# Early query sums for tiles 0 and 1, second-norm statistics by bn_stats, and new instruction orders in an attention-and-GLU block

## The chip, the cores and the metric

The kernel runs on one core of one Trainium2 chip. Its time is the device time of one execution in microseconds; the time before is 205.43 us, the median of 3 runs (205.39 to 205.56). The engines are PE (TensorE, with its weight loads shown as PEld), DVE (VectorE), ACT (ScalarE), POOL (GpSimd) and SP (SyncE, which only issues DMAs here). Each has its own queue of instructions and takes them in order. An instruction that waits for another engine holds up all that is queued behind it on its own.

## The reference

One transformer block on x of 2048 rows by 448 columns, bf16. First comes linear attention with 16 heads of 28 columns, and then a gated layer of width 1792:

```python
qkv = layernorm(x) @ wqkv
pq, pk = einsum(q, w_phi), einsum(k, w_phi)          # per head, 28 by 28
phi_q = concat([softmax(pq), softmax(-pq)])          # phi_k likewise
kv, z = einsum(phi_k, v), sum over rows of phi_k
o  = (phi_q @ kv) / (phi_q . z + 1e-6)
h  = x + o @ wo
g, u = layernorm(h) @ w_gate, layernorm(h) @ w_up
out = h + (sigmoid(g) * u) @ w_down
```

## The kernel before

The 2048 rows lie as 16 tiles of 128 rows. Every piece of work is an "op" with a name, an engine, and the keys of what it reads and writes (`Graph.op`). The engines' orders are written out by hand in the table ORDER, one list of op names for each engine. `emit` walks these lists, and puts a semaphore wait wherever an op needs what another engine, a DMA, or a nearby op of its own engine writes. So the rows of an engine's timeline stand in the order of its list, and each can be named from it; the names below are those of the list, with the tile number at the end (`ek4` is tile 4).

The head (to about 47 us) works as follows. A tile of x comes in (`x`), bn_stats and bn_aggr give its mean and variance (`bst`, `agg`), POOL makes the reciprocal root (`ve1`, `pow1`, with `nm1` and `nb1`), and `xn` writes the normed tile. `xn` may stand on ACT, DVE or POOL. A transpose follows (`xT`), for tiles 0 to 3 on PE with an evacuation `xTe`, for the others by a DMA that SP issues. There are three buffers for the normed tile, so `xn` of tile t waits for the transpose of tile t-3. PE multiplies by the folded key weights and by the value weights: `pva`, `pvb` for one tile from tile 4 on (`ppa` to `vvb` for tiles 0 to 3), into PSUM banks t%2 and 2+t%2. The a part and the b part use opposite halves of the array. ACT takes the exponentials of the key projection with both signs (`ek`, two instructions), ACT or DVE copies the values (`v1`), DVE sums the exponentials by head (`ss`, a tensor_reduce) and inverts the sums (`rs`). `phi` is the product of exponentials and inverse sums, a tensor_tensor on POOL or DVE, into three buffers. PE adds phi transposed times values into banks 6 and 7 (`kva`, `kvb`). `kvz` A to D masks that result into SBUF; `kvzones` writes a column of ones of each head beforehand, from `mask2`, whose two columns are the parity of the partition. `w2m1` and `w2e1` fold the query weights, which need the four transposed loads `ld_q`. `pqa`, `pqb` project the queries of four tiles at once, in two halves, and `eq` takes their exponentials with both signs in two instructions.

The tail of the attention, per tile: `num` (16 small matmuls of eq with kvz, into two banks) gives numerators, denominators and, by the ones column, the sums of the query exponentials. On DVE, `rsm` inverts the negative-sign sum, `qq` is the ratio of sums, `b` scales, `c` adds, `rden` inverts the denominator, and `o` (DVE or POOL) divides. Then `oT` transposes, `woa` and `wob` project with wo for two tiles, `h` adds x. For tiles 0 and 1 x is added on PE, by an identity matmul, and `h` is an ACT copy that accumulates the row sum. `sq` (ACT) accumulates the squares, `nm`, `ve`, `pow2` make mean and reciprocal root, `hn` norms, `hT` transposes (on PE for tiles 0 and 1). From there on PE works on `ga`, `gb` (gate and up, first for tiles 0 and 1), `d..` (down), with the attention of the later tiles between.

The places that the text speaks of: the list ORDER; `kvzones`, `xnorm`, `ekv` (`ek`, `ss`, `rs`, `phi`), `pq` (the function `eqf` with both exps), `kvmask`, `num`, `resid`, `wout`, and PROGRAM, which sets the order in which the ops of the tail are recorded.

## Time and profile before

| what | us |
|---|---|
| median of 3 runs | 205.43 |
| the profiled execution | 205.5 |
| its span, first to last instruction | 203.7 |
| PE busy | 197.6 (97%) |
| DVE busy | 135.9 (67%) |
| ACT busy | 96.5 (47%) |
| POOL busy | 56.8 (28%) |
| granted TensorE clock | 1.00 |

The shares are means over stages that differ. By windows of 4 us, DVE is busy 4.00 us in each window from 20 to 40, POOL 2.38 to 4.00 and ACT 3.43 to 4.00, and PE 3.31 to 4.00. From 96 us on PE is busy 4.00 us in nearly each window, DVE 0 to 3.9, POOL mostly 0. A row of the timeline shows the start in us, the duration in us, the engine, the line of the kernel, the operation, what it writes and reads with shapes, the number of instructions merged in it, and in square brackets the idle time before it with what ended that. A busy PE is not PE at its peak: matmuls overlap, and two that use opposite halves of the array run side by side (a pair of 448 columns starts every 0.19 us, though each shows 0.35).

### The profile page before, as it was taken

Reading aid. Unit: us, or ns where it says so; the run is one execution under the profiler, and the core shown is the slowest. Engines: PE = TensorE matmul, PEld = TensorE weight load, DVE = VectorE, ACT = ScalarE, POOL = GpSimd, SP = SyncE. Lnnn points to the kernel's source line nnn. Section 1 sums busy time; section 2 is a strip of 40 time slices with the busy share of each in tenths; the row PEclk is TensorE's granted clock in tenths of the full one; section 3 lists DMA queues with packets and bytes.
Section 4 is the critical chain, followed back from the end, with each engine's and each line's share of the span. In section 5 each row is a group of like instructions: output and inputs, shape, how many; then the busy total and the mean of one; then the engine's idle time right before and its main releaser. Section 6 shows DMA issues by size and latency. Waiting matters only on the chain.

```text
span 203.7 us, 5832 instructions
## 1 busy us (share of the span) xinstructions
PE 197.6 (97%) x2476; PEld 109.8 (54%) x2476; DVE 135.9 (67%) x329; ACT 96.5 (47%) x194; POOL 56.8 (28%) x98
## 2 busy tenths in 40 slices
...
GB/s 151 318 140 122 55 80 55 245 309 345 196 52 55 65 89 28 55 81 0 3 0 80 122 29 26 3 74 24 58 40 56 3 0 3 0 0 138 0 0 90
DMA packets 32866, 16.25 MB, mean 80 GB/s; under 512 B 25096, under 2 KB 31944, under 8 KB 32840
## 3 DMA queue, kind: packets, MB, share of 16 engines
...
q8 instruction: 19, 0.31, 0.7%
...
q14 instruction: 7, 0.06, 0.1%
...
## 4 chain that ended last, share of the span: by engine, by line
PE 78%; DVE 9%; POOL 4%; DMA 3%; ACT 2%; issue 1%; SPq 1%; POOLq 0%
PE psum L298 73%; PE psum L875 5%; DMA x_sb<-in_A_x_dram 3%; DVE c_sb L746 1%; DVE b_sb L743 1%; POOL rst L516 1%; DVE st L503 1%; DVE xn_pad L532 1%; DVE ss L634 1%; POOL phi L644 1%; DVE rsm L740 1%; ACT xn_pad L529 1%; SPq L397 1%; DVE o_pad L752 1%; ACT v L489 0%
## 5 line engine op out<-in xcount | busy, mean ns | idle before, releaser
L298 PE MATMUL psum<-xnT,wg_sb 64*128 64x512 bf16 (+1 forms) x490 | 93.3, 333 | 0.4 <-DVE rsm L740 0.3
L298 PE MATMUL psum<-xnT,wu_sb 64*128 64x512 bf16 (+1 forms) x490 | 93.2, 333 | 0.0
L847 ACT ACTIVATE sg_sb<-psum 128x512 bf16<-128x512 f32 (+1 forms) x70 | 35.0, 511 | 91.2 <-PE psum L298 90.7
L848 DVE SCALAR_TENSOR_TENSOR hhT<-sg_sb,psum 128x512 bf16<-128x512 bf16 (+1 forms) x70 | 38.9, 576 | 53.9 <-ACT sg_sb L847 53.2
L298 PEld LDWEIGHTS psum<-xnT,wg_sb 64*128 64x128 bf16 x490 | 44.4, 94 | 23.8 <-DVE hhT L848 4.7
L298 PEld LDWEIGHTS psum<-xnT,wu_sb 64*128 64x128 bf16 x490 | 44.4, 94 | 13.4
L298 PE MATMUL psum<-wd_sb,hhT 64*128 64x448 bf16 x336 | 36.8, 349 | 0.0
L298 PEld LDWEIGHTS psum<-wd_sb,hhT 64*128 64x128 bf16 x336 | 17.2, 94 | 15.0 <-DVE x_sb L774 0.6
L644 POOL TENSOR_TENSOR phi<-hhT,rs 128x896 bf16<-128x896 bf16 x14 | 23.3, 1688 | 2.4 <-DVE rs L640 1.9
L298 PE MATMUL psum<-Wk,xnT 64*128 64x448 bf16 x112 | 22.5, 350 | 0.5 <-ACT Wk L489 0.2
L298 PE MATMUL psum<-wv_sb,xnT 64*128 64x448 bf16 x112 | 22.5, 351 | 0.1
L782 POOL TENSOR_SCALAR ve<-ssq 128x1 f32<-128x1 f32 x14 | 3.0, 212 | 65.2 <-ACT junk L779 65.0
L634 DVE TENSOR_REDUCE ss<-hhT 128x32 f32<-128x896 bf16 x16 | 16.9, 1059 | 0.1
L298 PE MATMUL psum<-xnT,Wq 64*120 64x512 bf16 x112 | 14.7, 384 | 0.1
L298 PE MATMUL psum<-wo_o,oT 64*128 64x448 bf16 x56 | 13.2, 349 | 0.0
L298 PE MATMUL psum<-wo_e,oT 64*128 64x448 bf16 x56 | 13.1, 349 | 0.0
L875 PE MATMUL psum<-wd_sb,hhT 128*128 128x448 bf16 (+2 forms) x70 | 11.2, 316 | 0.0
L882 DVE SCALAR_TENSOR_TENSOR x_sb<-psum,x_sb 128x448 bf16<-128x448 f32 (+2 forms) x17 | 9.4, 592 | 2.2 <-PE psum L875 1.6
L779 ACT ACTIVATE junk<-x_sb,sum 128x448 bf16<-128x448 bf16 x16 | 10.5, 658 | 0.0
L503 DVE BATCH_NORM_STATS2 st<-x_sb 128x6 f32<-128x448 bf16 x16 | 9.4, 607 | 1.7 <-DMA x_sb<-in_A_x_dram 1.6
L298 PEld LDWEIGHTS psum<-Wk,xnT 64*128 64x128 bf16 x112 | 7.6, 94 | 5.4 <-PE psum L298 0.5
L746 DVE TENSOR_TENSOR c_sb<-b_sb,psum 128x464 bf16<-128x464 bf16 x16 | 10.1, 633 | 0.4
...
## 6 DMA issues: line engine op xcount, KB each, us to landing
...
```

What stands on the lines that cost most here:

```text
L298: p = e.matmul(o, lhsT=w, rhs=r, start=st, stop=sp, tile_position=(row, 0))
L397: return op(eng, name, lambda e: e.dma_start(dst, src), r=r, w=w, dma="in" if eng == "sp" else "ain", nring=48 if eng == "sp" else 8, kb=kb)
L503: op("dve", "bst%d" % t, lambda e: e.bn_stats(st1[:, t, :], x_sb[:, t, :]), r=[("x", t)], w=[("st1", t)])
L634: op("dve", "ss%d" % t, lambda e: e.tensor_reduce(ss[:, s, :].rearrange("p (b h) -> p b h", h=2), eks.rearrange("p b (d h) -> p b h d", h= ...
L644: return e.tensor_tensor(phi[:, sp, :, :, :].rearrange("p b a n -> p (b a) n")[:, :, 0:56].rearrange("p b (d h) -> p b d h", h=2), eks.rea ...
L746: op("dve", "c%d" % t, lambda e: e.tensor_tensor(h3(c_sb), h3(b_sb), OPv[:, :, :, 0:EV], ALU.add), r=K("b") + BB, w=K("c"))
L779: op("act", "sq%d" % t, lambda e: e.activation(junk[:, t % 2, :], h_sb[:, t, :], ACT.Square, bias=sum2[:, t:t + 1], scale=-float(D), accum ...
L782: op(("pool", "dve"), "ve%d" % t, lambda e: e.tensor_scalar(ve2[:, t:t + 1], ssq2[:, t:t + 1], 1.0 / D ** 3, EPS, op0=ALU.mult, op1=ALU.ad ...
L847: op("act", "sig" + nm, lambda e: e.activation(sg_sb[:, k, 0:N], bk(bg)[:, 0:N], ACT.Tanh, scale=0.5), r=[B(bg)], w=[("sg", k)])
L848: op("dve", "hh" + nm, lambda e: e.scalar_tensor_tensor(out=hhT[(t0 // 4) % NHH][:, ff, ns], in0=sg_sb[:, k, 0:N], scalar=1.0, in1=bk(bu)[ ...
L875: p = e.matmul(bk(b)[:, lo:hi], lhsT=hb[:, ff, TS(t)], rhs=wd_sb[:, ff, lo:hi], start=ff == 0, stop=ff == FT - 1)
L882: op("dve", "fin%d%s" % (t, nm), lambda e: e.scalar_tensor_tensor(out=h_sb[:, t, lo:hi], in0=bk(b)[:, lo:hi], scalar=0.5, in1=h_sb[:, t, l ...
```

## The change

Four edits, and orders that go with them.

- A new op `qs`: 32 matmuls of `eq` for tiles 0 and 1 with the new two-column tile `par` (mask2 in bf16) give the sums of the query exponentials of both tiles without kvz, in banks 2 and 3. One `rsm0` and one `qq0` then serve both tiles; `rsm1` and `qq1` go. `num` makes them itself from tile 2 on.
- For tiles 0 and 1, `h` is a plain copy on ACT; bn_stats (`bs2`) reads the PSUM bank on DVE before it, bn_aggr (`ag2`) gives mean and variance, `ve` adds epsilon on POOL, and `hn` subtracts the mean on DVE. `sq` and `nm` of these tiles go.
- `eq` is two ops (p and m) in place of one with two instructions.
- The memsets `epsl0`, `epsr0`, `v1ones` stand earlier on POOL.
- In the lists: `xn8` goes from DVE to POOL, `xn10` from DVE to ACT, `xn14` from ACT to POOL, `xn15` from ACT to DVE (`xn9` stays on DVE), `kvzones` from DVE to ACT. `phi8`, `phi12` and `phi14` go from POOL to DVE, `phi10` from DVE to POOL. The `v1` copies are shared out anew. `o2` goes from DVE to POOL, `o6`, `o7` from POOL to DVE. Weight loads move ahead of and between the transposes on SP. PE's order differs from `ppa0` to `dn0_11`.

The lists, up to where the first gate matmuls stand, and the head of the code:

```diff
     "sp": (
-        "x1 x0 ld_k0 x2 ld_k2 x4 x6 ld_v0 x10 ld_v2 x8 ld_q2 ld_q1 ld_q0 x12 ld_q3 xT4 xT5 x14 xT6 xT7 xT8 xT9 "
-        "xT10 xT11 xT12 xT13 xT14 xT15 ld_wg0 ld_wu1 ld_wu3 ld_wd1 ld_wg1 ld_woe0 ld_wu0 ld_woe1 ld_woo0 ld_woo1 "
...
+        "x1 x0 ld_k0 x2 ld_k2 x4 x6 ld_v0 x10 ld_v2 x8 ld_woe1 ld_wu0 ld_q2 ld_q1 ld_q0 ld_wg1 x12 ld_woo1 ld_q3 "
+        "xT4 xT5 x14 xT6 ld_wd2 xT7 xT8 ld_wd5 ld_wg2 xT9 xT10 ld_wd4 ld_wd0 xT11 ld_wd3 xT12 xT13 xT14 xT15 "
+        "ld_woo0 ld_wg3 ld_wg0 ld_woe0 ld_wu3 oT2 ld_wu2 ld_wu1 ld_wd6 oT3 ld_wd1 oT4 oT5 oT6 oT7 hT2 hT3 oT8 oT9 "
...
     "act": (
-        "wphi3 wphi2 wphi1 wphi0 wTe0 wTe1 xT1e xT0e wTe2 w2e0_0 w2e0_1 w2e0_2 w2e0_3 xn3 xn4 ek0 ek1 xn5 v1_0 "
-        "v1_1 xn6 ek2 v1_2 v1_3 ek3 w2e1_1 ek4 v1_4 ek5 v1_5 w2e1_0 v1_6 ek6 xn11 ek7 v1_7 xn12 ek8 xn13 ek9 "
-        "w2e1_3 w2e1_2 ek10 xn14 ek11 xn15 v1_11 ek12 eq0_0 ek13 ek14 ek15 v1_14 eq0_1 kvzB eq1_0 eq1_1 eq2_0 oT0e "
-        "eq2_1 h1 h0 sq1 sq0 eq3_0 eq3_1 sig0_1 sig0_0 sig0_3 sig0_2 sig0_5 sig0_4 sq2 sig0_7 sig0_6 sq3 sig0_9 "
...
+        "wphi3 wphi2 wphi1 wphi0 wTe0 wTe1 xT1e xT0e wTe2 w2e0_0 w2e0_1 w2e0_2 w2e0_3 xn3 par xn4 ek0 ek1 xn5 v1_0 "
+        "xn6 ek2 ek3 v1_2 w2e1_0 v1_3 w2e1_1 ek4 v1_4 w2e1_2 ek5 xn10 ek6 v1_6 xn11 ek7 w2e1_3 ek8 v1_8 xn12 ek9 "
+        "xn13 ek10 v1_10 ek11 v1_11 ek12 kvzones eq0_0p ek13 eq0_0m ek14 ek15 v1_15 v1_14 eq0_1p eq0_1m eq1_0p "
+        "kvzB eq1_0m eq1_1p eq1_1m eq2_0m oT1e eq2_0p eq2_1p eq2_1m h1 h0 eq3_0m eq3_0p eq3_1p eq3_1m sig0_1 "
...
     "pe": (
...
-        "ppa0 warm9 ppb0 vva0 xT3 xT2 vvb0 ppa2 ppb2 vva2 vvb2 w2m1_1 w2m1_0 seed kva0 pva4 kvb0 pvb4 pva5 kva1 "
-        "pvb5 kvb1 pva6 kva2 pvb6 pva7 w2m1_2 w2m1_3 pvb7 pva8 kvb2 kva3 pvb8 kvb3 pva9 kva4 pvb9 kvb4 pva10 kva5 "
-        "pvb10 pva11 kvb5 kva6 pvb11 pqa0_0 pva12 kvb6 kva7 pvb12 kvb7 pqb0_0 kva8 pva13 kvb8 kva9 pvb13 kvb9 "
-        "kva10 pva14 pvb14 kvb10 pva15 kva11 pvb15 pqa0_1 kvb11 kva12 pqb0_1 pqa1_0 kvb12 kva13 kvb13 kva14 kvb14 "
-        "kva15 kvb15 pqb1_0 pqa1_1 num0 num1 pqb1_1 pqa2_0 num2 pqb2_0 pqa2_1 oT0 oT1 pqb2_1 num3 woa0 wob0 num4 "
-        "pqa3_0 pqb3_0 num5 pqa3_1 pqb3_1 hT1 hT0 num6 ga0_1 ga0_0 gb0_1 gb0_0 num7 woa2 ga0_3 ga0_2 gb0_3 gb0_2 "
...
+        "ppa0 warm9 xT3 ppb0 xT2 vva0 vvb0 ppa2 ppb2 vva2 seed vvb2 w2m1_1 w2m1_0 kva0 pva4 kvb0 pvb4 pva5 w2m1_2 "
+        "pvb5 kva1 pva6 kvb1 kva2 pvb6 pva7 kvb2 pvb7 kva3 pva8 w2m1_3 pvb8 pva9 kvb3 kva4 pvb9 kvb4 pva10 pqa0_0 "
+        "pvb10 kva5 pva11 kvb5 kva6 pvb11 pva12 kvb6 kva7 pvb12 kvb7 kva8 pqb0_0 pva13 kvb8 kva9 pvb13 pva14 kvb9 "
+        "kva10 pvb14 pva15 kvb10 kva11 pvb15 pqa0_1 kvb11 kva12 pqb0_1 kvb12 kva13 pqa1_0 kvb13 kva14 pqb1_0 kvb14 "
+        "kva15 kvb15 qs pqa1_1 num0 pqb1_1 num1 pqa2_0 num2 pqb2_0 pqa2_1 oT0 oT1 pqb2_1 num3 woa0 wob0 num4 "
+        "pqa3_0 pqb3_0 pqa3_1 num5 hT1 pqb3_1 hT0 num6 ga0_1 ga0_0 gb0_1 gb0_0 woa2 num7 ga0_3 ga0_2 gb0_3 gb0_2 "
...
     "dve": (
...
-        "bst10 agg11 bst9 bst7 agg6 agg7 agg9 bst8 agg8 agg10 mask2 xT3e xT2e ss0 nm1_8 nm1_6 rs0 ss1 bst13 rs1 "
-        "bst12 ss2 bst14 rs2 agg14 xn8 ss3 agg13 agg12 rs3 xn9 bst15 ss4 agg15 xn10 ve1_12 ss5 rs4 ss6 rs5 ss7 rs6 "
-        "v1_8 ss8 v1_9 rs7 ss9 rs8 v1_10 ss10 rs9 rs10 kvzones ss11 v1_12 rs11 phi10 ss12 v1_13 rs12 ss13 rs13 "
-        "ss14 rs14 v1_15 ss15 rs15 phi15 kvzC kvzD kvzA rsm0 qq0 rsm1 b0 qq1 c0 b1 rden0 c1 rsm2 rden1 qq2 o1 b2 "
-        "c2 oT1e rden2 rsm3 qq3 b3 c3 o2 rden3 rsm4 qq4 b4 c4 ve1 rsm5 qq5 ve0 hn1 rden4 b5 c5 hT1e hT0e rsm6 qq6 "
...
+        "bst11 agg11 agg10 agg7 mask2 bst8 bst6 bst9 agg6 agg8 agg9 ve1_6 xT2e ve1_8 xT3e ss0 v1_1 rs0 ss1 bst13 "
+        "rs1 ss2 bst12 agg13 ss3 agg12 rs2 bst15 bst14 rs3 agg15 agg14 v1_5 xn9 nm1_12 ss4 ss5 rs4 v1_7 ss6 rs5 "
+        "ss7 rs6 ss8 v1_9 rs7 ss9 rs8 rs9 ss10 xn15 phi8 ss11 rs10 v1_12 rs11 ss12 v1_13 rs12 ss13 phi12 rs13 ss14 "
+        "rs14 ss15 phi14 rs15 phi15 kvzA kvzC kvzD rsm0 qq0 b0 c0 b1 rden0 c1 rsm2 rden1 qq2 o1 b2 c2 oT0e rden2 "
+        "rsm3 qq3 b3 c3 rden3 bs2_1 rsm4 ag2_1 qq4 bs2_0 b4 ag2_0 c4 hn1 rden4 rsm5 qq5 hT1e b5 hn0 c5 hT0e rden5 "
...
     "pool": (
-        "neghalf ident0 ident phipad wqpad nm1_1 pow1_1 ve1_0 pow1_0 nm1_2 ve1_2 ve1_3 pow1_3 nm1_3 pow1_2 nb1_3 "
-        "ve1_4 nm1_4 pow1_4 nb1_4 nb1_2 xn2 opad0 ve1_6 pow1_6 ve1_8 v1ones epsl0 epsr0 pow1_8 nb1_6 phi0 nb1_8 "
-        "xn7 phi1 phi2 phi3 nm1_12 pow1_12 nb1_12 phi4 phi5 phi6 phi7 phi8 phi9 phi11 phi12 phi13 phi14 o0 nm1 o3 "
...
+        "neghalf ident0 ident phipad wqpad epsl0 epsr0 nm1_1 pow1_1 ve1_0 pow1_0 nm1_2 ve1_2 ve1_3 pow1_3 v1ones "
+        "nm1_3 pow1_2 nb1_3 ve1_4 nm1_4 pow1_4 nb1_4 nb1_2 opad0 xn2 pow1_6 nm1_6 nb1_6 nm1_8 pow1_8 nb1_8 phi0 "
+        "xn7 xn8 phi1 phi2 ve1_12 phi3 pow1_12 phi4 nb1_12 phi5 phi6 xn14 phi7 phi9 phi10 phi11 phi13 o0 o2 ve1 o3 "
+        "pow2_1 ve0 pow2_0 o4 o5 nm2 nm3 pow2_2 hn2 pow2_3 hn3 o9 pow2_4 ve7 ve5 pow2_7 pow2_5 nm5 ve6 pow2_6 ve8 "
...
-    "pq:0,0,4 pq:0,1,4 kvz pq:1,0,0 pq:1,1,4 pq:2,0,0 num:0 num:1,1,2 ot:0 ot:1 wo:0 pq:2,1,4 pq:3,0,0 num:2 "
+    "pq:0,0,4 pq:0,1,4 qs:2 kvz pq:1,0,0 pq:1,1,4 pq:2,0,0 num:0 num:1,1,2 ot:0 ot:1 wo:0 pq:2,1,4 pq:3,0,0 num:2 "
...
+        par = sb("par", [P, 2])
+        st2 = sb("st2", [P, 2, 6], f32)
+        mv2 = sb("mv2", [P, 2, 2], f32)
...
+        op(("dve", "act"), "par", (lambda e: e.tensor_copy(par[:], mask2[:]), lambda e: e.copy(par[:], mask2[:])), r=["mask2"], w=["par"])
```

The functions:

```diff
-            def eqf(e):
-                e.activation(eq[c][:, 0, 2 * i:2 * i + 2, :].rearrange("p g n -> p (g n)"), src, ACT.Exp)
-                return e.activation(eq[c][:, 1, 2 * i:2 * i + 2, :].rearrange("p g n -> p (g n)"), src, ACT.Exp, scale=-1.0)
-            op("act", "eq%d_%d" % (c, i), eqf, r=[B(b), B(b + 1)], w=[("eq", c, i)])
+            for sg in range(2):
+                op("act", "eq%d_%d%s" % (c, i, "pm"[sg]), lambda e, sg=sg: e.activation(
+                    eq[c][:, sg, 2 * i:2 * i + 2, :].rearrange("p g n -> p (g n)"), src, ACT.Exp, scale=1.0 - 2.0 * sg),
+                   r=[B(b), B(b + 1)], w=[("eq", c, i, sg)])
 
         for t in range(0, NV2, 2):
             proj2("vv", t, 2, wv, wv_keys)
@@ -714,6 +719,22 @@
                     return p
                 op(("dve", "act"), "kvz" + k, (f, fa), r=[B(6 + a), "mask2"], w=["kvz" + k])
 
+        def qsum(b):
+            def f(e):
+                def part(half, x):
+                    return [(bk(b + x)[:, (t * 16 + (sg * G + gg) * 2):(t * 16 + (sg * G + gg + 1) * 2)], eq[0][half, sg, gg, TS(t)],
+                             par[half, :], True, True) for t in range(2) for sg in range(2) for gg in range(G)]
+                return both(e, part(QL, 0), part(QH, 1))
+            op("pe", "qs", f, r=[("eq", 0, k, sg) for k in range(2) for sg in range(2)] + ["par"], w=[B(b), B(b + 1)], rows=64, half={b: 0, b + 1: 1})
+            ov = psum[:, b * 512:(b + 2) * 512].rearrange("p (a n) -> p a n", a=2)[:, :, 0:32].rearrange("p a (t x) -> p t a x", t=2)
+
+            def h4(ap):
+                return ap[:, 0:2, :].rearrange("p t (a h) -> p t a h", a=2)
+
+            op("dve", "rsm0", lambda e: e.reciprocal(h4(rsm), ov[:, :, :, 8:16]), r=[B(b), B(b + 1)], w=[("rsm", 0), ("rsm", 1)])
+            op("dve", "qq0", lambda e: e.tensor_tensor(h4(qq), h4(rsm), ov[:, :, :, 0:8], ALU.mult),
+               r=[("rsm", 0), ("rsm", 1), B(b), B(b + 1)], w=[("qq", 0), ("qq", 1)])
+
         def num(t, n=1, b=6):
             s, NB = t % NS, 2 * n
             for i in range(n):
@@ -722,7 +743,7 @@
                         return [(bk(b + x)[:, (sg * G + gg) * 2 * E:(sg * G + gg + 1) * 2 * E], eq[t // 4][half, sg, gg, TS(t)],
                                  kvz[half, x if sg == x else 2, gg, :], True, True) for sg in range(2) for gg in range(G)]
                     return both(e, part(QL, 0), part(QH, 1))
-                op("pe", "num%d" % (t + i), f, r=[("eq", (t + i) // 4, k) for k in range(2)] + KVZ,
+                op("pe", "num%d" % (t + i), f, r=[("eq", (t + i) // 4, k, sg) for k in range(2) for sg in range(2)] + KVZ,
                    w=[B(b + 2 * i), B(b + 2 * i + 1)], rows=64, half={b + 2 * i: 0, b + 2 * i + 1: 1})
             ov = psum[:, b * 512:(b + NB) * 512].rearrange("p (a n) -> p a n", a=NB)
             OPv = ov[:, :, 0:8 * E].rearrange("p a (h e) -> p a h e", e=E)
@@ -737,9 +758,10 @@
 
             def K(k):
                 return [(k, s + i) for i in range(n)]
-            op("dve", "rsm%d" % t, lambda e: e.reciprocal(h2(rsm), OMv[:, :, :, E - 1]), r=BB, w=K("rsm"))
-            op("dve", "qq%d" % t, lambda e: e.tensor_tensor(h2(qq), h2(rsm), OPv[:, :, :, E - 1], ALU.mult),
-               r=K("rsm") + BB, w=K("qq"))
+            if t >= 2:
+                op("dve", "rsm%d" % t, lambda e: e.reciprocal(h2(rsm), OMv[:, :, :, E - 1]), r=BB, w=K("rsm"))
+                op("dve", "qq%d" % t, lambda e: e.tensor_tensor(h2(qq), h2(rsm), OPv[:, :, :, E - 1], ALU.mult),
+                   r=K("rsm") + BB, w=K("qq"))
             op("dve", "b%d" % t, lambda e: e.tensor_tensor(h3(b_sb), OMv[:, :, :, 0:EV],
                                                            h2(qq)[:, :, :, None].to_broadcast([P, NB, 8, EV]), ALU.mult),
                r=K("qq") + BB, w=K("b"))
@@ -768,26 +790,32 @@
         def resid(t, b, ha=False):
             c, s = t // 4, t % NH
             if ha:
-                op("act", "h%d" % t, lambda e: e.activation(h_sb[:, t, :], bk(b)[:, 0:D], ACT.Identity, accum_out=sum2[:, t:t + 1]),
-                   r=[B(b)], w=[("x", t), ("sum2", t)])
+                st = op("dve", "bs2_%d" % t, lambda e: e.bn_stats(st2[:, t % 2, :], bk(b)[:, 0:D]), r=[B(b)], w=[("st2", t)])
+                op(("act", "dve"), "h%d" % t, (lambda e: e.copy(h_sb[:, t, :], bk(b)[:, 0:D]),
+                                               lambda e: e.tensor_copy(h_sb[:, t, :], bk(b)[:, 0:D])), r=[B(b)], w=[("x", t)], after=[st])
+                op("dve", "ag2_%d" % t, lambda e: e.bn_aggr(mv2[:, t % 2, :], st2[:, t % 2, :]), r=[("st2", t)], w=[("mv2", t)])
+                op(("dve", "pool"), "ve%d" % t, lambda e: e.tensor_scalar(ve2[:, t:t + 1], mv2[:, t % 2, 1:2], 1.0, EPS, op0=ALU.mult,
+                                                                          op1=ALU.add), r=[("mv2", t)], w=[("ve2", t)])
             else:
                 op("dve", "h%d" % t, lambda e: e.scalar_tensor_tensor(out=h_sb[:, t, :], in0=bk(b)[:, 0:D], scalar=1.0, in1=x_sb[:, t, :],
                                                                       op0=ALU.mult, op1=ALU.add, accum_out=sum2[:, t:t + 1]),
                    r=[B(b), ("x", t)], w=[("x", t), ("sum2", t)])
-            op(("dve", "pool"), "nm%d" % t, lambda e: e.tensor_scalar(nm2[:, t:t + 1], sum2[:, t:t + 1], -1.0 / D, None, op0=ALU.mult),
-               r=[("sum2", t)], w=[("nm2", t)])
-            op("act", "sq%d" % t, lambda e: e.activation(junk[:, t % 2, :], h_sb[:, t, :], ACT.Square, bias=sum2[:, t:t + 1],
-                                                         scale=-float(D), accum_out=ssq2[:, t:t + 1]),
-               r=[("x", t), ("sum2", t)], w=[("junk", t % 2), ("ssq2", t)])
-            op(("pool", "dve"), "ve%d" % t, lambda e: e.tensor_scalar(ve2[:, t:t + 1], ssq2[:, t:t + 1], 1.0 / D ** 3, EPS, op0=ALU.mult, op1=ALU.add),
-               r=[("ssq2", t)], w=[("ve2", t)])
+            if not ha:
+                op(("dve", "pool"), "nm%d" % t, lambda e: e.tensor_scalar(nm2[:, t:t + 1], sum2[:, t:t + 1], -1.0 / D, None, op0=ALU.mult),
+                   r=[("sum2", t)], w=[("nm2", t)])
+                op("act", "sq%d" % t, lambda e: e.activation(junk[:, t % 2, :], h_sb[:, t, :], ACT.Square, bias=sum2[:, t:t + 1],
+                                                             scale=-float(D), accum_out=ssq2[:, t:t + 1]),
+                   r=[("x", t), ("sum2", t)], w=[("junk", t % 2), ("ssq2", t)])
+                op(("pool", "dve"), "ve%d" % t, lambda e: e.tensor_scalar(ve2[:, t:t + 1], ssq2[:, t:t + 1], 1.0 / D ** 3, EPS, op0=ALU.mult, op1=ALU.add),
+                   r=[("ssq2", t)], w=[("ve2", t)])
             op("pool", "pow2_%d" % t, lambda e: e.tensor_tensor(rst2[:, t:t + 1], ve2[:, t:t + 1], neghalf[:, 0:1], ALU.pow),
                r=[("ve2", t), "neghalf"], w=[("rst2", t)])
 
             def hnf(e):
                 return e.tensor_scalar(hn_pad[:, s, :].rearrange("p (a f) -> p a f", a=2), windows(h_sb[:, t, :]),
-                                       nm2[:, t:t + 1], rst2[:, t:t + 1], op0=ALU.add, op1=ALU.mult)
-            op(("dve", "pool"), "hn%d" % t, hnf, r=[("x", t), ("nm2", t), ("rst2", t)], w=[("hn", s)])
+                                       mv2[:, t % 2, 0:1] if ha else nm2[:, t:t + 1], rst2[:, t:t + 1],
+                                       op0=ALU.subtract if ha else ALU.add, op1=ALU.mult)
+            op("dve" if ha else ("dve", "pool"), "hn%d" % t, hnf, r=[("x", t), ("mv2", t) if ha else ("nm2", t), ("rst2", t)], w=[("hn", s)])
             if t < 2:
                 pe_transpose("hT%d" % t, [hn_pad[:, s, kt * P:(kt + 1) * P] for kt in range(KT)], b, hnT[c][:, :, TS(t)],
                              ("hn", s), ("xnT", t))
```

2 lines of the change are left out of this document (added), and 37 rows, old and new, of the table ORDER.

## The prediction

> **What bounds the kernel now.** I read the chain of waits first, then the busy time by windows, then the timelines of DVE and POOL. The steady part needs little reading. From the first gate matmul on, the chain of waits is PE alone:
>
> ```profile
> 60.50 0.42 DVE xnT L489
> ...
> 61.13 4.88 PE psum L298 x86
> 66.01 0.04 issue
> 66.05 9.43 PE psum L298 x172
> 75.48 0.04 issue
> 75.52 51.16 PE psum L298 x686
> 126.68 0.01 issue
> 126.69 57.47 PE psum L298 x558
> ```
>
> So the end follows the start of ga0_1 (61.13 us), with 203.7 - 61.1 = 142.6 us of matmuls behind it that the change keeps. What counts is when ga0_1 starts. Two stretches lead to it. The first is the DVE chain behind num0, which ends at 47.41 ("issue" lines are the few hundredths between a release and the next start):
>
> ```profile
> 47.41 0.02 issue
> 47.44 0.27 DVE rsm L740
> 47.70 0.02 issue
> 47.73 0.17 DVE qq L741
> 47.90 0.17 DVE rsm L740
> 48.07 0.51 DVE b_sb L743
> ```
>
> DVE stays on this chain to 57.4 us and again at 60.5, with POOL and PE between. The second is the head, in which PE, DVE and POOL are all nearly full. In the windows, DVE is busy 4.00 of 4 us in each window from 20 to 40 us. PE waits there for phi4 (27.7 to 28.64) and at the end for phi15, which DVE finishes at 44.86. But some of DVE's full time is not work:
>
> ```profile
> 19.72 2.16 DVE L532 TENSOR_SCALAR xn_pad<-x_sb,nm,rst 128x512 bf16<-128x512 bf16 x1
> ...
> 23.19 0.31 DVE L532 TENSOR_SCALAR xn_pad<-x_sb,nm,rst 128x512 bf16<-128x512 bf16 x1
> ...
> 34.44 0.81 DVE L434 CAST kvz<-mask 128x24 bf16<-128x24 f32 x1
> ```
>
> ```profile
> 18.40 3.33 POOL L644 TENSOR_TENSOR phi<-hhT,rs 128x896 bf16<-128x896 bf16 x2
> 23.34 1.70 POOL L644 TENSOR_TENSOR phi<-hhT,rs 128x896 bf16<-128x896 bf16 x1 [1.62 <-DVE rs L640]
> ```
>
> The same operation takes 0.31 us (xn9) with POOL idle and 2.16 (xn8) with POOL in phi1 and phi2; it ends 0.16 after phi2 (21.72). kvzones ends 0.08 after phi8 (35.17). So some DVE operations wait for POOL's running one, and POOL's next can come first if it was ready earlier: phi2 was ready at 19.76 (its rs2), before xn8's turn at 19.80; phi9 was ready only at 34.74 (kvb6), after kvzones' at 34.51, and kvzones went first.
>
> **The change part by part.** Times after the change are estimates: the queues walked in their new order with durations from rows. A "spacing" is start to start of neighbours, shorter than the duration by about 0.08.
>
> *The tail, num0 to ga0_1.* I keep num0 at 47.0. (a) rsm0, qq0 leave the chain, since qs gives their sums from eq0 alone; rsm1, qq1 go. qs is 32 small matmuls. The 32 of num0 and num1 take 0.46 us to the next start, 0.63 with the pipeline; the floor is 0. I take 0.55. It stands behind kvb15, where PE waits for kvz anyway (kvb15 45.27, pqb1_0 and pqa1_1 fill to 46.94, kvzA ends 46.85); pqb1_0 moves ahead of kvb14, so qs and pqa1_1 (0.85) fill 1.4 of the 1.4 us. Without that cover it would cost 0.5. b0 starts at num0's end, 47.45, not 47.98: -0.53. That holds through o1, b2, c2; oT0e ends 52.5 (oT1e before: 53.01), woa0 starts 52.6 (53.12), wob0 ends 54.7 (55.24). (b) Now DVE pays: two bn_stats. From PSUM they have no row; the SBUF ones take 0.59 (spacing 0.51), a 448-wide copy from PSUM (v1) 0.55, h2 from PSUM 0.62. So 0.51 to 0.65, I take 0.55 spacing. Two bn_aggr at 0.1 to 0.17, and hn0 (0.33) come from POOL's and ACT's side; o2 (0.55) goes to POOL, ve0 and ve1 (0.15) too. In turn from bs2_1 at 54.75: rsm4 55.28, ag2_1 55.45, qq4 55.55, bs2_0 55.65, b4 56.2, ag2_0 56.75, c4 56.9 to 57.53. ve1 on POOL now waits for ag2_1 (55.62); queued behind it are o3 (0.94, so oT3) and pow2_1, which ends at 57.6. hn1 57.65 to 58.05, rden4, rsm5, qq5 to 58.55, hT1e 58.55, b5 58.88, hn0 59.42, c5 59.75 to 60.38, hT0e 60.3 to 60.72. ga0_1 starts at 60.93: -0.2, of the 0.53 won in front. The gap of 0.44 that DVE has before rsm5 today is gone: this stretch is then DVE without a break. (c) The copies h1, h0 (0.54) wait for bs2_1, bs2_0. Behind them on ACT stand eq3's exps, which end at 61.2 (61.60 before). These have slack, as does sq (0.85 each), which goes. The split of the exps keeps both 0.91; it lets kvzB stand between them, at 46.1 to 46.7, before kvzA ends. The order behind ga0_1 I cost at nothing, as PE covers it: hT2 lands today at 77.83, about 0.7 before ga2_1, and hn2 goes from DVE's 73.65 to POOL behind pow2_2.
>
> *The head.* (a) par and kvzones go to ACT; no row has such a small copy there, so between 0.19 (an accumulator read) and 0.4 (kvzB's half, 0.3, and a little). I take 0.2 for par, which makes xn4 0.2 later; xT4 has 2.9 us of slack. Memsets: epsl, epsr leave the 0.79 us at 13.98 to 14.73 in front of pow1_8 for POOL's idle time at 2.0 to 3.7. v1ones goes ahead of nm1_3 for 0.1. phi0 wins nothing: rs0 is later (15.9, was 15.33), since v1_1 (0.5) stands before it and xT2 waits for xn2 (now behind opad0, 0.35). PE runs xT2 ahead of vva0, so vva0 slips from 11.90 to 13.05. PE's drains and waits behind it take that up again (vvb0, ppa2 and seed waited too): kva0 at 18.3, as before. pva4 is 0.3 late by v1_2, now behind ek3. (b) Loads. SP issues ld_woe1, ld_wu0, ld_wg1, ld_woo1 (784 KB, 4 issues of 0.5) ahead of xT4, and six ld_wd and ld_wg2 between the xT. At the 318 GB/s of the second slice, 784 KB is 2.5 us. Today ld_q3 lands at 15.07, xT4 15.62, x14 18.86, and they are wanted at 17.3, 18.5 and 18.9; so 0 to +0.5, I take 0, as this time has half-empty slices (DMA share 0.46 at 12 to 16) and bst15 moves back to 20.7. The late loads get 2 us slack: ld_wu2 and ld_wu1 stand behind oT2, which waits for o2 (53.7), and land by 58.5 for 60.9. (c) DVE from ss0 to phi15: 13.86 to 44.86 today, 31.0 us, of which 1.75 (xn8) and 0.65 (kvzones) are blocked and 0.35 waits; work 28.25. Added: phi8, phi12, phi14 less phi10, +0.96; xn15 +0.25. Gone: xn8 0.25, xn10 0.3, kvzones 0.15 (to ACT, which idles 0.16 to 0.7 before each ek there). Six v1 copies stay six. Net +0.4 with the small ones: 28.65, from 14.1: 42.75. Waits for ek9, ek10 and others add 0.8: 43.55, or -1.3, if nothing is blocked. (d) New blocking. xn9 and xn15 stay on DVE and three phi come, all beside POOL's phi. xn15's turn is 33.15 (ss10 waits for ek10, 32.05), in phi7 (31.85 to 33.55); it goes at 33.55. phi9 is ready at 33.65 (kvb6), and phi8's turn is 33.75. If phi8 is an operation that waits for POOL, it goes at 35.45: 1.6 us in which DVE stands and, on PE, kva8 and behind it pqb0_0 and pva13. phi12 and phi14 find POOL waiting for rs13 or idle.
>
> Does a DVE tensor_tensor wait? One row speaks: o1 (0.66) beside POOL's o0 ends 0.48 after o0, where o2, with POOL idle, takes 0.62. I take yes. The Trainium skill, SBUF — State Buffer, "Who interferes with whom", says that a DVE instruction with two SBUF inputs contends with a GpSimd instruction that reads SBUF, and that the one to issue first holds the port for its whole length. By that rule it waits; o1's row agrees, by 0.04 us only. Without the rule the sum would stay at -1.3.
>
> With it: phi8 ends 35.9, ss11, rs10, v1_12, rs11, ss12, v1_13, rs12, ss13 follow (40.65), phi12 41.2, rs13, ss14, rs14, ss15 43.7, phi14 44.2, rs15, phi15 45.05: +0.2 against 44.86.
>
> *Sum.* The profiled execution took 205.5, its span 203.7; 1.8 lies around it, and it stands 0.07 over the median 205.43. Head +0.2, tail -0.2, and 0.1 for the loads: 205.5 + 0.1 = **205.6**, no change that can be told.
>
> **The rivals.** *A: nothing is blocked.* phi8 comes before phi9, by kvb6 being 0.15 later or phi7 ending 0.15 earlier, or tensor_tensor doesn't wait. For it: the margin is 0.1 us. Against: POOL runs phi4 to phi9 with hardly a gap. Head -1.3, tail -0.2: 204.0.
>
> *B: xn9 is blocked too; slower.* Its turn is 22.65; phi2 ends at 22.65 to 23.0, ve1_12 and phi3 follow without a gap. If xn9 comes after ve1_12 starts, phi3 goes first and xn9 at 24.8. ss4, ss5 and rs4 then end at 27.4, phi4 starts 27.45 (26.89 before), DVE ends ss5 at 27.1. From there 17.55 us of work and the block at phi8, now 2.1 (xn15 or phi8 behind a phi9 to 36.8): 46.75, +1.9. With the tail: 205.5 + 1.7 = 207.2. For it: xn8 does just this today. Against: phi3 can ask only once ve1_12 runs, and an xn9 that comes in phi2 is first.
>
> *C: xn9 blocked, phi8 not.* 27.1 + 17.55 = 44.65, -0.2; with the tail -0.4: 205.1.
>
> *D: the early sums bring nothing,* because qs waits for eq0_1m (ACT's 45.1) and kvzB for eq1_0p. If either is 0.5 late, num0 is, and the tail's -0.2 becomes +0.3: 206.0 on the forecast's head. ACT's queue (ek15, v1_15, v1_14, eq0_1p, eq0_1m, eq1_0p, kvzB) has only 0.15 to spare.
>
> **How the numbers follow.** Two races of about 0.1 us decide, which a walk can't settle. Forecast 0.35 (own range 205.1 to 206.1), A 0.22, B 0.25, C 0.10, D 0.08. From 204.0 to 207.0 holds all but half of A's lower and half of B's upper side, some 0.2. About 0.2% (0.41 us) is what a measurement tells from no change. Faster: A 0.22, C 0.08, 0.06 of the forecast: 0.36. Slower: B 0.25, D 0.06, 0.14 of the forecast: 0.45. Same: 0.19.
>
> **What would show it.** In DVE's timeline: phi8 of 0.55 or 2 us, xn9 of 0.31 or 2 us. phi15's end at 45.05 (A 43.55, B 46.75). b0 right at num0's end; DVE without a gap from bs2_1 to hT0e; ga0_1 13.9 us behind num0's start (14.14 today). bn_stats at 0.55 to 0.65. It is wrong if PE waits for ld_q3 or xT4 before 18.5, or if the 142.6 us behind ga0_1 change by more than 0.2.

## The result and the profile after

The changed kernel takes 206.55 us, the median of 4 runs (206.32 to 206.93), where the kernel before takes 205.41 on the same chip (205.02 to 205.56): 1.0069 of it, with a 95% interval of 1.005 to 1.0087. It is slower, by 1.1 us. The time lies within the range forecast, 0.95 over the value. The profiled execution took 206.67 us, its span 204.9. Times of single ops below are rows of the two traces, named by the lists.

| us | before | forecast | after |
|---|---|---|---|
| rs4 ends / phi4 starts | 26.72 / 26.89 | | 27.46 / 27.54 |
| xT11 lands / pva11 starts | 29.73 / 31.28 | | 33.33 / 33.47 |
| phi15 ends | 44.86 | 45.05 | 46.20 |
| num0 starts | 46.99 | 47.0 | 48.34 |
| num0 to ga0_1, start to start | 14.14 | 13.9 | 14.15 |
| ga0_1 to the end | 142.6 | 142.6 | 142.4 |

So the loss is all in the head (1.35 us at num0), the tail wins nothing, and what follows gives back 0.2. Two things happen in the head. The first is in DVE's timeline of the kernel after (start, duration, engine, line, operation, what it writes and reads, number of instructions, idle time before it):

```profile
22.76 0.63 DVE L494 CAST v<-psum 128x448 bf16<-128x448 f32 x1 [0.52 <-PE psum L299]
23.30 1.84 DVE L537 TENSOR_SCALAR xn_pad<-x_sb,nm,rst 128x512 bf16<-128x512 bf16 x1
25.06 0.16 DVE L519 TENSOR_SCALAR nm<-mv 128x4 f32<-128x4 f32 x1
25.13 2.07 DVE L639 TENSOR_REDUCE ss<-hhT 128x32 f32<-128x896 bf16 x2
27.12 0.34 DVE L645 RECIPROCAL rs<-ss 128x32 bf16<-128x32 f32 x1
```

and in POOL's:

```profile
23.09 0.25 POOL L516 TENSOR_SCALAR ve<-mv 128x4 f32<-128x4 f32 x1
23.30 1.69 POOL L649 TENSOR_TENSOR phi<-hhT,rs 128x896 bf16<-128x896 bf16 x1
24.95 1.08 POOL L521 TENSOR_TENSOR rst<-ve,neghalf 128x4 f32<-128x4 f32 x1
27.54 1.69 POOL L649 TENSOR_TENSOR phi<-hhT,rs 128x896 bf16<-128x896 bf16 x1 [1.51 <-DVE rs L645]
```

xn9 (L537) takes 1.84 us and ends 0.15 after POOL's phi3: it is blocked, as xn8 was before. Its turn came at 23.30, not at 22.65, since v1_5 ahead of it had waited 0.52 for PE; by then phi3 was ready as well. Behind xn9 stand ss4, ss5 and rs4, and phi4 waits for rs4 while POOL idles 1.51 us. The second thing is in the timeline of SP, whose rows are DMA issues:

```profile
27.71 1.09 SPq L401 DMA_DIRECT2D wd_sb<-in_B_w_down_dram  x2
28.85 1.19 SPq L547 DMA_TRANSPOSE xnT<-xn_pad  x1
30.08 0.58 SPq L401 DMA_DIRECT2D wd_sb<-in_B_w_down_dram  x1
30.71 6.58 SPq L547 DMA_TRANSPOSE xnT<-xn_pad  x4
```

The transpose at 28.85 (xT11) stands behind two loads of 224 KB. In the kernel before, the row of that stretch holds transposes alone (xT8 to xT13):

```profile
21.90 8.66 SPq L542 DMA_TRANSPOSE xnT<-xn_pad  x6
```

xT11 lands 4.5 us after its issue began, where that of the kernel before, with no load near it, took 3.1. Who waits for it is seen further on in POOL's timeline of the kernel after:

```profile
33.50 0.77 POOL L537 TENSOR_SCALAR xn_pad<-x_sb,nm,rst 128x512 bf16<-128x512 bf16 x1 [0.83 <-DMA xnT<-xn_pad]
34.23 1.69 POOL L649 TENSOR_TENSOR phi<-hhT,rs 128x896 bf16<-128x896 bf16 x1
36.71 3.33 POOL L649 TENSOR_TENSOR phi<-hhT,rs 128x896 bf16<-128x896 bf16 x2 [0.80 <-DVE phi L649]
```

and in DVE's:

```profile
35.02 1.04 DVE L537 TENSOR_SCALAR xn_pad<-x_sb,nm,rst 128x512 bf16<-128x512 bf16 x1 [0.45 <-DMA xnT<-xn_pad]
35.99 0.61 DVE L649 TENSOR_TENSOR phi<-hhT,rs 128x896 bf16<-128x896 bf16 x1
```

xn14 (33.50) waits for the buffer that xT11 reads, and holds up phi7 behind it on POOL; xn15 (35.02) waits for the transpose after it, and is then blocked by phi7 until 35.92. PE's pva11 waits for xT11 as well (landed at 33.33):

```profile
33.47 0.35 PE L299 MATMUL psum<-Wk,xnT 64*128 64x448 bf16 x1 [0.92 <-ACT hhT L636]
```

The row names ACT's ek10, which ends at 33.46, but the weight load of this matmul had begun at 33.44, before that end. phi8 (35.99) is not blocked. POOL's phi9 is: the buffer that it writes was free at 36.28 (kvb6 had read it), its inputs were ready long before, and it starts at 36.71, 0.11 after phi8's end.

The chain of waits of the kernel after, from wob0's end to ga0_1 (start, duration, what):

```profile
55.40 0.95 PE psum L299 x8
...
56.37 0.63 DVE st L793
...
57.31 0.19 POOL ve L797
...
57.58 0.94 POOL o_pad L774
58.51 0.52 POOL rst L811
...
59.06 0.41 DVE hn_pad L815
...
60.33 0.63 DVE b_sb L765
60.96 0.32 DVE hn_pad L815
61.28 0.55 DVE c_sb L768
61.83 0.37 DVE xnT L494
```

bn_stats from PSUM (st, 0.63) starts as wob0 ends. But o3 (o_pad, 0.94) stands on POOL ahead of pow2_1 (rst), and b5 and c5 stand on DVE ahead of hn0 and hT0e.

### The profile page after: what moved, and what is told of

Its sections match the earlier page's. It is cut to its first block, busy times and chain, and to the rows that moved or that the text cites. A ratio compares the mean times of both kernels' runs of the same rounds, so it can differ in the third digit from the quotient of the medians.

```text
span 204.9 us, 5889 instructions
## 1 busy us (share of the span) xinstructions
PE 197.3 (96%) x2508; PEld 111.3 (54%) x2508; DVE 137.5 (67%) x328; ACT 95.3 (46%) x189; POOL 55.4 (27%) x99
## 3 DMA queue, kind: packets, MB, share of 16 engines
HBM read 8.34 MB, written 1.84 MB: 50 GB/s over the span
## 4 chain that ended last, share of the span: by engine, by line
PE 85%; DVE 4%; DMA 4%; POOL 3%; ACT 2%; issue 1%; SPq 1%; POOLq 0%
PE psum L299 79%; PE psum L903 5%; DMA x_sb<-in_A_x_dram 2%; DMA xnT<-xn_pad 1%; DVE xn_pad L537 1%; POOL rst L521 1%; ACT hhT L635 1%; ACT hhT L636 1%; SPq L401 1%; DVE st L508 1%; PE psum L501 0%; POOL o_pad L774 0%; POOL xn_pad L537 0%; DVE hn_pad L815 0%; DVE b_sb L765 0%
## 5 line engine op out<-in xcount | busy, mean ns | idle before, releaser
L649 POOL TENSOR_TENSOR phi<-hhT,rs 128x896 bf16<-128x896 bf16 x12 | 20.1, 1688 | 3.2 <-DVE rs L645 2.3
L809 POOL TENSOR_SCALAR ve<-ssq 128x1 f32<-128x1 f32 x11 | 2.2, 204 | 51.8 <-ACT junk L806 51.3
L685 ACT ACTIVATE eq<-psum 120x1024 bf16<-120x1024 f32 x16 | 15.8, 1027 | 0.9 <-PE psum L299 0.7
L774 POOL TENSOR_TENSOR o_pad<-c_sb,rden 128x448 bf16<-128x448 bf16 x8 | 7.5, 935 | 19.0 <-DVE rden L770 18.8
L765 DVE TENSOR_TENSOR b_sb<-psum,qq 128x464 bf16<-128x464 f32 x16 | 10.2, 637 | 0.3
```

The lines of the kernel that those rows point to most:

```text
L649: return e.tensor_tensor(phi[:, sp, :, :, :].rearrange("p b a n -> p (b a) n")[:, :, 0:56].rearrange("p b (d h) -> p b d h", h=2), eks.rea ...
L685: op("act", "eq%d_%d%s" % (c, i, "pm"[sg]), lambda e, sg=sg: e.activation(eq[c][:, sg, 2 * i:2 * i + 2, :].rearrange("p g n -> p (g n)"), ...
L765: op("dve", "b%d" % t, lambda e: e.tensor_tensor(h3(b_sb), OMv[:, :, :, 0:EV], h2(qq)[:, :, :, None].to_broadcast([P, NB, 8, EV]), ALU.mul ...
L774: return e.tensor_tensor(o_pad[:, t % NO, off:off + D].rearrange("p (h d) -> p h d", h=H), c_sb[:, t % NS, :, 0:DH], rden[:, t % NS, :][:, ...
L809: op(("pool", "dve"), "ve%d" % t, lambda e: e.tensor_scalar(ve2[:, t:t + 1], ssq2[:, t:t + 1], 1.0 / D ** 3, EPS, op0=ALU.mult, op1=ALU.ad ...
```

## The experiments

Each time is a median, beside the ratio to the kernel before on the same chip and its 95% interval. Line numbers of the variants differ by a few, as the lists are wrapped anew.

**Loads and xn9, first try.** Three variants of the kernel after: with the order of loads of before (all behind xT15), with xn9 ahead of v1_5 on DVE, with both.

```diff
 sp
-"... x8 ld_woe1 ld_wu0 ld_q2 ... ld_wg1 x12 ld_woo1 ... xT6 ld_wd2 xT7 xT8 ld_wd5 ld_wg2 xT9 xT10 ld_wd4 ld_wd0 xT11 ld_wd3 xT12 ..."
+"... x8 ld_q2 ... x12 ... xT6 xT7 xT8 xT9 xT10 xT11 xT12 xT13 xT14 xT15 ld_wg0 ld_wu1 ... ld_wd0 ld_wu2 oT2 ..."
 dve
-"... agg14 v1_5 xn9 nm1_12 ss4 ss5 rs4 ..."
+"... agg14 xn9 v1_5 nm1_12 ss4 ss5 rs4 ..."
```

> The changed kernel with the weight loads on SP back behind xT15, as before the change. Theory D (the loads ahead of and between the transposes make xT9, xT11 and xT12 land late, 28.20, 33.33 and 35.00 us, and PE and POOL wait for them): pva11 starts by about 32.4 instead of 33.47, xn14 no longer waits on POOL, num0 comes at about 47.4 instead of 48.34, time near 205.6. Rival L (the stall of DVE in xn9 alone decides, since DVE is the bound from there to phi15): num0 stays within 0.3 of 48.34, time 206.3 to 206.6.

> The changed kernel with two neighbours on DVE exchanged: xn9 ahead of v1_5, so that it asks at about 22.25 us, while POOL is in phi2, and not at 23.3, when phi3 has begun. Theory L (a waiting DVE operation goes after the POOL operation that runs, unless POOL's next was ready earlier): xn9 ends 0.1 to 0.2 after phi2 (23.0), rs4 ends near 26.0 instead of 27.46, phi4 starts near 26.1 instead of 27.54, time 205.6 to 206.2, less if the late transposes do not hold it. Rival (xn9 is slow by itself or waits for a buffer): it still lasts near 1.8 us, rs4 stays at 27.4. If theory D holds as well, pva11 still waits for xT11 at 33.3 and the gain is mostly lost again.

> Both edits: loads behind xT15, xn9 ahead of v1_5. If L and D are both real and one hides the other, this gains more than the sum of the two alone: num0 at 46.3 to 46.8, time 204.6 to 205.1, under the kernel before. If only one is real, it equals that one's run.

| | time | ratio | xn9 | rs4 ends | xT11 lands | num0 | ga0_1 |
|---|---|---|---|---|---|---|---|
| loads as before | 206.11 | 1.0047 (1.0017 to 1.0077) | 22.97 to 24.64 | 26.95 | 29.70 | 47.05 | 64.35 |
| xn9 first | 206.52 | 1.006 (1.0038 to 1.0082) | 21.94 to 23.21 | 27.32 | 31.04 | 48.02 | 62.15 |
| both | 206.10 | 1.0039 (1.0019 to 1.0059) | 21.84 to 22.66 | 26.77 | 28.67 | 46.89 | 62.02 |

(The profiled execution of the first was its longest, 208.54 us. PE's granted clock there is 0.50 from 52 to 54 us, behind a stand of 1.8 us, where that of the third stays at 1.00 behind a shorter one; so the first one's ga0_1 stands for that execution only.) The loads bring num0 back by 1.3 us, but only 0.4 of the time; xn9 alone brings nothing. Each has its own reason. In the second, xT11 lands at 31.04 with the same loads ahead of it, and it is xT12 (34.73) that pva12 waits for (34.87). DVE's timeline shows where the block went:

```profile
21.94 1.27 DVE L534 TENSOR_SCALAR xn_pad<-x_sb,nm,rst 128x512 bf16<-128x512 bf16 x1
23.14 0.61 DVE L491 CAST v<-psum 128x448 bf16<-128x448 f32 x1
23.67 1.42 DVE L516 TENSOR_SCALAR nm<-mv 128x4 f32<-128x4 f32 x1
25.00 2.07 DVE L636 TENSOR_REDUCE ss<-hhT 128x32 f32<-128x896 bf16 x2
```

xn9, asked for within phi2, goes as phi2 ends. But now nm1_12, an operation on four columns, is the one that meets phi3, takes 1.42 us, and holds ss4 in its place. In the third, with num0 at 46.89, the chain of waits has a hole in PE:

```profile
46.89 2.29 PE psum L296 x52
49.17 1.25 issue
50.42 1.85 PE psum L296 x24
```

"issue" means that PE waits for nothing that the profile shows, for 1.25 us in the middle of num2; in the first variant's profile it stands there from 49.3 to 51.1. This ate most of what the head had won, and the time expected for this variant (204.6 to 205.1) was missed; what goes with the hole comes below.

**Before's head with after's tail.** All queues as before up to phi15, ek12, pqb0_1 and ld_wu2, and as after behind these; par on ACT behind ek1.

> The kernel before up to kva12, phi15 and ek12, its loads too, with the change from there on: qs, bn_stats for tiles 0 and 1, split exps, the new orders of the tail. My sum said that num0 to ga0_1 falls from 14.14 to 13.9 us: 205.2. What the changed kernel's profile shows (14.15) says no gain: 205.4 with num0 at 47.0. Either way the head's loss (num0 1.35 later) must be gone; if the time stays above 206, the loss comes from the tail's edits (DVE load of bn_stats, waits of POOL) after all.

Time 205.85, 1.0032 (1.0011 to 1.0052). The profiled execution took 204.94, the shortest of its ten. In it num0 starts at 46.44 and ga0_1 14.16 us later. So in this execution the tail is neutral, within 0.02 us of both kernels (14.14 and 14.15). By the median the variant is 0.3% slower than the kernel before, though its head in that trace is 0.55 us earlier, and both times expected (205.2 and 205.4) were missed. Why the other nine runs (205.43 to 206.51) are longer, their traces would have to tell, and there are none; so that the tail costs nothing in the median is not shown.

**The block with nm1_12 away, and five loads.** Three more variants of the kernel after: xn9 first and nm1_12 behind rs4; only the five loads between xT8 and xT12 moved behind ld_wu3 (the five earlier ones stay); both.

```diff
 dve
-"... agg14 v1_5 xn9 nm1_12 ss4 ss5 rs4 v1_7 ..."
+"... agg14 xn9 v1_5 ss4 ss5 rs4 nm1_12 v1_7 ..."
 sp
-"... xT8 ld_wd5 ld_wg2 xT9 xT10 ld_wd4 ld_wd0 xT11 ld_wd3 xT12 ... xT15 ld_woo0 ld_wg3 ld_wg0 ld_woe0 ld_wu3 oT2 ..."
+"... xT8 xT9 xT10 xT11 xT12 ... xT15 ld_woo0 ld_wg3 ld_wg0 ld_woe0 ld_wu3 ld_wd5 ld_wg2 ld_wd4 ld_wd0 ld_wd3 oT2 ..."
```

> After, with xn9 ahead of v1_5 on DVE and nm1_12 (DVE's small subtraction for the last group) behind rs4 in place of ahead of ss4. In the run with xn9 alone moved, xn9 went at 21.94, but nm1_12 then took 23.67 to 25.08 and ended 0.02 after POOL's phi3. Theory 'the block is handed on to the next DVE operation of that kind': with nm1_12 away too, ss4 starts near 23.8, rs4 ends by 26.2 and phi4 starts by 26.4 (after: 27.46 and 27.54; xn9 alone: 27.32 and 27.40). Rival 'rs4 waits for ACT's or PE's work, not for POOL': rs4 stays at 26.9 to 27.3. The loads are left as in after, so xT11 still lands near 33 and num0 starts no earlier than 47.5; time 206.0 to 206.5 by either theory.

> After, with only the five loads ld_wd5, ld_wg2, ld_wd4, ld_wd0, ld_wd3 moved from between the xT transposes to behind ld_wu3; xn9 and nm1_12 stay, so xn9 is still blocked until 25.1 and phi4 starts near 27.5. It completes the square of after (206.55), xn9 and nm1_12 alone (207.05) and both (204.94). Theory 'two limits in series, the phi chain and the transposes': with the transposes free xT11 lands by 31, num0 starts at 47.1 to 47.7 (1.1 us of late phi4, of which the chain behind takes some back), time 205.4 to 206.0. Rival 'the five loads are all of it': num0 at 46.7 and 204.9 to 205.1, as with both. Third 'only both together bring anything': 206.3 to 206.6.

> The same, and the five loads ld_wd5, ld_wg2, ld_wd4, ld_wd0, ld_wd3 go from between the xT transposes to behind ld_wu3; the five early ones stay ahead. Theory 'the five between delay the late xT': xT11 lands by 31, pva11 starts by 31.6, num0 starts at 46.0 to 46.8 (after 48.34), and since only ten loads, not fifteen, stand behind xT15, PE does not stand still in num2: time 204.6 to 205.4. Rival 'the loads cost the same wherever they stand, behind xT15 as PE's stall in num2 of 1.4 to 1.8 us': num0 is early but ga0_1 no earlier than 61.8, time 205.8 to 206.3. Third: the five early loads delay the xT, not these: xT11 stays near 33, time 206.0 to 206.5.

| | time | ratio | rs4 ends | phi4 | xT12 lands | pva12 | num0 | ga0_1 |
|---|---|---|---|---|---|---|---|---|
| after | 206.55 | 1.0069 (1.005 to 1.0087) | 27.46 | 27.54 | 35.00 | 35.19 | 48.34 | 62.49 |
| xn9, nm1_12 | 207.05 | 1.0092 (1.0072 to 1.0112) | 25.71 | 25.79 | 34.97 | 35.10 | 48.16 | 62.32 |
| five loads | 205.47 | 1.0013 (0.9997 to 1.0028) | 27.28 | 27.36 | 34.17 | 34.30 | 47.45 | 61.81 |
| both | 204.94 | 0.9987 (0.9974 to 1.0) | 25.94 | 26.02 | 33.53 | 33.66 | 46.72 | 60.88 |

With nothing that can be blocked ahead of rs4, phi4 comes 1.75 us earlier, as the theory of the handed-on block said; the rival (rs4 at 26.9 to 27.3) falls. Alone it wins nothing, since the transposes then set pva12 (35.10 against 35.19). Its median of 207.05 lies over the 206.0 to 206.5 expected; the profiled execution, at 206.50, was its shortest, and no trace tells what the longer ones do. The loads alone win 1.1 us, and both 1.6, which is more than the change had lost. So the head has two limits in series, the phi chain and the transposes, and moving five loads away eases the second but does not lift it: pva12 starts 0.13 us behind the landing of xT12 in all of these variants. In the variant with the loads alone, DVE's timeline shows the race between xn9 and phi3 go the other way:

```profile
22.52 0.63 DVE L491 CAST v<-psum 128x448 bf16<-128x448 f32 x1 [0.52 <-PE psum L296]
23.07 0.41 DVE L534 TENSOR_SCALAR xn_pad<-x_sb,nm,rst 128x512 bf16<-128x512 bf16 x1
23.39 1.66 DVE L516 TENSOR_SCALAR nm<-mv 128x4 f32<-128x4 f32 x1
```

Here xn9 came just before phi3 (23.16) and took 0.41; nm1_12 behind it took the block, 1.66 us, and rs4 is no earlier than in the kernel after.

**A gap on POOL in the kernel before.** Its own xn8 stood 2.16 us. One memset moves:

```diff
 pool
-"... xn2 opad0 ve1_6 ... xn7 phi1 phi2 phi3 ..."
+"... xn2 ve1_6 ... xn7 phi1 opad0 phi2 phi3 ..."
```

> Before, with one POOL operation moved: the memset opad0 (0.35 us) stands between phi1 and phi2. Before's own times lie in two groups (11 of 28 at 204.72 to 205.05, 17 at 205.36 to 206.14). Theory 'the groups are the toss at the handover from phi1 to phi2: xn8, which waits since 19.72, goes first or stands until 21.8': with the gap xn8 always goes first, in 0.4 to 1.0 us, rs3 ends by 22.2 and phi3 starts by 22.3 (before 23.34), all times lie at 204.4 to 205.1 with a median near 204.8. Rival 'the groups come from elsewhere (DMA, PE)': xn8 is free but the times still lie in two groups 0.6 apart, median 205.2 to 205.5. Third: xn8 stands until phi2's end though there is a gap (a memset holds too): phi3 at 23.3 or later, median 205.4 to 205.8.

Time 204.63 (204.46 to 205.11, 12 runs), 0.9977 (0.9963 to 0.999). All but one of its runs lie under 204.9, where the kernel before on that chip has 15 of 24 under 205.2 and 9 at 205.45 to 205.94. POOL's timeline of this variant:

```profile
18.02 1.68 POOL L642 TENSOR_TENSOR phi<-hhT,rs 128x896 bf16<-128x896 bf16 x1
19.65 0.20 POOL L418 MEMSET o_pad<- 128x128 bf16 x1
19.79 0.20 POOL L419 MEMSET o_pad<- 128x128 bf16 x1
19.96 3.42 POOL L642 TENSOR_TENSOR phi<-hhT,rs 128x896 bf16<-128x896 bf16 x2
```

and DVE's:

```profile
19.61 0.53 DVE L530 TENSOR_SCALAR xn_pad<-x_sb,nm,rst 128x512 bf16<-128x512 bf16 x1
20.06 1.07 DVE L632 TENSOR_REDUCE ss<-hhT 128x32 f32<-128x896 bf16 x1
```

xn8 slips in during the memsets, rs3 ends at 21.52 (before 23.26), and phi3 follows phi2 without the 1.62 us of idle time; num0 starts at 46.06, 0.93 earlier. The theory of the toss (that either of the two can go first, from run to run) holds, in the times too. But the move does a second thing: with no memset in front of ve1_6, POOL's phi1 starts 0.38 us earlier (18.02, before 18.40). So of the 0.93 at num0 some 0.55 is left for xn8, as much as before's head with after's tail shows with the memset in its old place (num0 at 46.44). The times say the same: the 15 shorter runs of the kernel before have a median of 204.92, 0.3 over this variant's. In the variant with before's head above, whose POOL queue has no such gap, xn8 won by itself (19.88 to 20.25).

**Orders in the tail.** Before's head and after's tail again, with POOL's o3 ahead of ve1, on DVE ag2_0 ahead of b4, hn1 ahead of c4, hn0 ahead of rsm5, hT0e ahead of b5, and on PE hT0 ahead of pqb3_1.

```diff
 pool
-"... o2 ve1 o3 pow2_1 ..."
+"... o2 o3 ve1 pow2_1 ..."
 dve
-"... qq4 bs2_0 b4 ag2_0 c4 hn1 rden4 rsm5 qq5 hT1e b5 hn0 c5 hT0e rden5 ..."
+"... qq4 bs2_0 ag2_0 b4 hn1 c4 rden4 hn0 rsm5 qq5 hT1e hT0e b5 c5 rden5 ..."
```

> Before's head with after's tail (as in the run b1_tail, num0 to ga0_1 14.16 us there, DVE: bs2_1 rsm4 ag2_1 qq4 bs2_0 b4 ag2_0 c4 hn1 ...), and only orders in the tail changed: on POOL o3 ahead of ve1; on DVE ag2_0 ahead of b4, hn1 ahead of c4, hn0 ahead of rsm5, hT0e ahead of b5; on PE hT0 ahead of pqb3_1. Theory 'the 0.26 us that the early sums win is given back by what stands ahead of hn0 and pow2_1 in the queues': num0 to ga0_1 falls to 12.7 to 13.4 us, and the time by as much, to 0.8 to 1.3 us under b1_tail's run. Rival 'the tail is filled by PE and DVE work whatever its order': num0 to ga0_1 stays at 13.9 to 14.2. Third: ga0_1 comes earlier, but the gate stage then waits for what was put back (b5, c5, num6, pqb3_1), and the time behind ga0_1 grows from 142.5 to over 143.

Time 206.01, 1.005 (1.003 to 1.007). hT0e does end earlier (59.56), but num0 to ga0_1 is 15.05: PE stands 0.70 in num2, and then in front of num6, which waits for c5 (60.78) and has ga0_1 queued behind it. So this variant settled nothing, and three more followed, with the gap at phi2 in the head. The first has loads moved out of the way of the hole in num2, the second the tail's orders as well, with num6 behind gb0_0 and hh0_1, hh0_0 ahead of rsm6.

> Before's head with opad0 between phi1 and phi2 (the run e1_gap, 204.63), after's tail (qs, bn_stats, split exps), and loads set so that DMA is empty when PE asks for its instructions: behind xT15 only the two parts of each wo and the first two of w_gate and w_up, the other eleven behind oT3 to oT6. In the runs with before's loads and qs, PE's fetch of 16 KB, asked for at its instruction 1237, came 1.8 to 4.0 us late, and instruction 1475 (in num2) ran 1.48 to 1.51 us behind the fetch's end in the three runs that stood still there. Theory 'qs shortens the way to 1475 so that the late fetch shows': here the fetch is at most 0.5 us late, num2 takes 0.40, num0 to ga0_1 is 14.1 to 14.2, and the time is that of e1_gap, 204.4 to 204.9, where b1_tail (before's loads) had 205.85. Rival 'b1_tail's 0.5 us over before came from the tail's own work': 205.1 to 205.9 again. If the late loads are missed (dn0 near 76) or oT4 to oT6 come late behind them, the time behind ga0_1 grows over 142.8.

> The same with the tail's orders of b2_order, and on PE num6 behind gb0_0, on DVE hh0_1 and hh0_0 ahead of rsm6. In b2_order hT0e ended at 59.56 (12.72 us behind the start of num2's predecessor num0 at 46.39 is 59.11 without PE's 0.89 in num2), but ga0_1 stood on PE behind num6, which waits for c5 (60.78). Theory 'orders alone hold the tail': num0 to ga0_1 falls to 12.3 to 12.9, time 203.0 to 203.6. Rival 'what is put back costs the same behind ga0_1': ga0_1 comes that early, but gaps of PE in front of ga0_3 or woa2 take it back, time 204.2 to 205.0.

Both missed: 214.21 and 214.23 (1.0439, 1.0414 to 1.0464, and 1.0449, 1.0425 to 1.0473). The expectations took the loads of w_gate and w_up for blocks of columns; they are blocks of rows, and each gate matmul needs all eight, so ga0_1 waited for ld_wu3 until after 65. Ahead of that the traces can be read: num0 to hT0e's end is 13.84 us without the new orders and 12.79 with them (before 13.93, after 13.86). So the orders in the queues do hold back 1.05 us of hT0e. The last variant mends the loads, and puts num7 behind gb0_2 and hh0_3, hh0_2 ahead of rsm7.

> As the run g1_order (before's head with the gap at phi2, after's tail in new order), with two faults of g1 mended. There ga0_1 waited for ld_wu3 until 65.85, since each load of w_gate and w_up holds rows that every gate matmul needs: here all of them stand ahead of the tail again (wg1 and wu2 between the xT, ten loads behind xT15), and only the seven ld_wd, wanted at dn0_0 near 76, go behind oT3 to oT5. And num7 stood on PE ahead of ga0_3 and waited for c6: here it goes behind gb0_2, with hh0_3 and hh0_2 ahead of rsm7. Theory 'orders hold the tail, and a fetch that is late by 2.5 us at most shows in num2 by 0.4 at most': num0 to hT0e 12.7 to 13.2 (g0_tail 13.84, g1_order 12.79), ga0_1 at 59.1 to 59.7 (e1_gap 60.20), behind it 142.3 to 142.8, time 203.3 to 204.2. Rival 'what is put back costs the same behind ga0_1': ga0_1 as early, but gaps of PE ahead of ga0_3 or woa4 make it over 143, time 204.4 to 205.2. Third: PE stands 1 us or more at num2 behind a late fetch, time 204.4 to 205.2 with ga0_1 at 60.2 or later.

Time 207.22, 1.0104 (1.008 to 1.0129): the rival, worse than it said. ga0_1 starts at 59.62, 0.6 earlier than in the variant with the gap alone, but the chain of waits of this one goes on:

```profile
59.52 1.95 ACT eq L682 x2
61.46 0.05 issue
61.51 0.96 PE psum L296 x14
...
62.49 0.39 ACT sg_sb L872
...
62.90 0.75 DVE hhT L873 x2
```

The gate matmuls stop after their first eight (59.62 to 59.96), since the next ones write the banks that eq3_1p and eq3_1m are reading on ACT until 61.46, later now because pqb3_1 was put behind hT0. Behind that DVE takes hh, then b6, c6, b7, h2 and h3 in turn, and PE runs without a break again only from 69.08. The tail is held by three chains of nearly one length. In before's head with after's tail they end at 59.94 (c5, for num6), 60.31 (hT0e, for ga0_1, which starts at 60.60) and 60.81 (eq3_1m, for ga0_0, 61.04). In these runs, shortening one alone moved the wait to the next.

The fastest version that ran is the kernel before with the memset in the gap, 204.63. That is also the ratio furthest under 1 (0.9977); the kernel after with both mendings, 204.94, comes next, and their intervals overlap.

## Why the prediction was right and wrong

The measured 206.55 lies in the range of 204.0 to 207.0 and outside the 205.1 to 206.1 of the forecast's own case. What holds it is the part of the range kept for the rival B, while the loads that made most of the loss stand in none of the cases. To that extent the range was right by luck.

**Loads: the step that was mis-sized.** "So 0 to +0.5, I take 0." (The sum then carries 0.1 for them, and the list has five ld_wd between the xT, not six.) The reasons given were about ld_q3, xT4 and x14. The loads further on, among xT8 to xT12, were listed and not costed. They alone cost 1.1 us (206.55 less 205.47), more than the upper end of 0.5, and 2.1 with the phi chain free (207.05 less 204.94). The five early ones cost little: ld_q3 lands at 17.35 and xT4 at 18.08 (before 15.07 and 15.62), PE waits for neither, and xn7 on POOL stands 0.17 us for xT4. The variant that keeps them is at 204.94; no run moved them alone. Much of the price could have been read before: xT11 landed 1.55 us ahead of pva11 and xT12 3.3 us ahead of pva12, while the five loads ahead of xT12 hold 1,344 KB (four ld_wd of 224 KB and ld_wg2 of 448), an estimate of 4.1 us at the 332 GB/s that the windows of before show from 44 to 48 us.

A part of xT12's lateness is not the loads', and neither the forecast nor a rival looked at it. xn12 stands on ACT behind ek8 and v1_8 now. It ends at 30.66, where before, ahead of ek8, it ended at 27.79, and xT12 is issued only then. In the four variants with fewer loads among the transposes it still ends at 29.69 to 30.19, and xT12 lands at 33.53 to 34.17. So even with both mendings pva12 comes at 33.66, hardly earlier than before (33.70). No run moved xn12 alone.

**xn9: the rivals' mechanism, not the forecast's.** The forecast had xn9 free, with its turn at 22.65 inside phi2; the rivals B and C had it blocked, with rs4 at 27.4 and phi4 at 27.45. They came at 27.46 and 27.54. The step that failed is the turn: v1_5 ahead of xn9 waited for PE until 22.76. The argument used ("an xn9 that comes in phi2 is first") holds: at 21.94 it went as phi2 ended. What no case saw is that nm1_12 behind it takes the block over: phi4 starts at 27.40 with xn9 out of the way and at 25.79 with both.

**phi8: right about the wait, wrong about who waits.** A tensor_tensor with two SBUF inputs does shut POOL out: phi9, ready at 36.28, starts 0.11 after phi8's end at 36.60. The Trainium skill, SBUF — State Buffer, "Who interferes with whom", says that the port pair which the two engines share is an exclusive lock, and that issue order decides who blocks; the trace agrees, with POOL 0.43 us late here in place of DVE 1.6. It waits for POOL too, as forecast: phi12 starts at 41.44 beside POOL's phi11, takes 0.73 us and ends 0.48 after it, where phi14, with POOL idle, takes 0.61. phi8 came first because phi7 and with it kvb6 were late by the transposes. So the 1.6 us of the forecast were not lost there. By its conditions, xn9 blocked and phi8 not, C is the case that came, and its time of 205.1 is short by the loads (1.1) and by the tail's 0.2. phi15 ended at 46.20, between the forecast's 45.05 and B's 46.75.

**Tail: -0.2 forecast, 0 found.** b0 starts 0.66 us after num0's start (0.99 before, 0.45 forecast): rsm0 and qq0 no longer need num0, but they stand on DVE behind kvzD, which ends as num0 starts (48.28). Of the 0.53 forecast 0.33 came, and at wob0's end 0.26 is left (num0 to there 7.99, before 8.25). From there to hT0e's end it is 5.87, before 5.68 (forecast 6.02), and 0.08 more to ga0_1. So the step that failed in the tail is b0 right at num0's end. The prices were good: bn_stats from PSUM 0.63 (0.51 to 0.65), qs 0.54 with 0.41 to the next start (0.55), par 0.19 (0.2), kvzones on ACT 0.30 (0.2 to 0.4). D falls: qs and kvzB were not late, as num0 starts 0.06 after kvzD's end. A falls with xn9.

**Behind ga0_1:** 142.4 against 142.6, within the 0.2 allowed.
